# w_out's product with ELU's tile as the stationary operand: 384 and 192 moving columns in place of 512

## The chip, the cores and the metric

One core of a Trainium2 (trn2) chip. The metric is the device time of one execution in microseconds (us). Engines are named as in the profile: PE (TensorE's matmuls), PEld (its loads of stationary operands), DVE (VectorE), ACT (ScalarE), POOL (GpSimd), SP (SyncE, which issues most DMAs).

## What is computed

A softmax-weighted causal window of 7 tokens over x, head by head, then a two-layer network with ELU in between. Cut to what matters:

```
w = softmax(weight_gen, axis=-1)                  # 4 x 4096 tokens, 8 heads, 7 taps
out = einsum('bshk,bskhg->bshg', w, x_unf)        # x_unf: the last 7 tokens of x; 192 columns
x = out.reshape(16384, 192)
h = x @ w_in                                      # 192 -> 2048
g = np.where(h > 0.0, h, np.exp(np.minimum(h, 0.0)) - 1.0)
out = g @ w_out                                   # 2048 -> 192, float32
```

## The kernel before

The 16384 tokens are worked on in 32 blocks (`NB`) of 512 tokens (`N`). In a block, the 2048 inner columns are 16 tiles of 128 (`NF`), taken as 8 pairs (`NP`); one pair of one block is a step, 256 steps in all. A step does the product with w_in for its pair (two PSUM tiles `h`, one per f-tile), ELU on ACT and DVE, and, two steps later (`LAG`), the product with w_out.

Float32 accuracy at the price of fewer passes comes from splitting: x, w_in, ELU's result and w_out are each kept as a rounded part and a rest (`xhi`/`xlo`, `WI[..,0]`/`WI[..,1]`, `hi`/`lo`, the `O_HI`/`O_LO` columns of `WO`), in the type fp32r, and a product is rounded times rounded, rest times rounded and rounded times rest. Block 0 does without (`plain`): it uses float32 operands, each of whose matmuls shows as two records in the trace.

In blocks 1 to 31 (`APART`) each matmul contracts over one half of the partitions only (64 rows, `low` or `high`), and two such matmuls, one on each half, run side by side: a pair of matmuls. The product with w_in (`product_in`) is 9 matmuls of 512 columns for each of the two f-tiles. The product with w_out (`product_out`) has w_out's columns stationary and ELU's tile moving: five matmuls of 512 columns per f-tile and half, into the banks `acc` (output columns 0 to 127) and `accd` (columns 128 to 191 and the rest terms of columns 0 to 63), each half of the partitions with two banks of its own. `side` interleaves them: nine product_in matmuls of one half go beside product_out matmuls of the other. So a step is 19 pairs of matmuls of 512 columns. PSUM has eight banks: four `h`, four for the output.

When a block's sums are done, `drain` turns the four output banks over with DVE transposes (`turned`, L828), POOL adds the halves and the crossed columns (`plus`, L887), ACT copies the crossed columns (L847), and SP stores them in six DMAs of 128-byte rows (L839). Meanwhile POOL does the window sums of a later block (`conv`, L486 and L502), DVE the softmax, the transposes to `xt` and the split of x, and SP loads `wg` and `xw` (L431) and copies halves of `xhi` and `xlo` across the partitions (L634, L635).

The order on each engine is not written out: `Plan` gets every piece of work as a task with an engine, a cost, what it reads and writes and a due time, places the tasks in time and emits them in the order of their starts (`issue`). A task on the planner's "dma" engine is issued from SP's queue, in that order.

Of the kernel before, what the change touches and what calls it, by code (L numbers as in the profile page):

```python
# [52 lines left out]
class Plan:  # L53
# [7 lines left out]
    HOP = {"dma": 2200, "pe": 250, "act": 220, "dve": 220, "pool": 220}  # L61
    SAME = {"dma": 0, "pe": 0, "act": 60, "dve": 60, "pool": 60}
# [71 lines left out]
def conv_elu_kernel(  # L134
# [11 lines left out]
    nc = tc.nc  # L146
# [18 lines left out]
    D1 = D - P  # L165
# [13 lines left out]
    FIRST = (0, 2700, 5400, 12000, 18400, 28600, 38200, 44600, 51000, 56900, 62800)  # L179
# [22 lines left out]
    WO = const.tile([P, NF, 3 * P], F32R, name="WO")  # L202
    O_HI, O_BOTH, O_LO = (slice(c, c + P) for c in range(0, 3 * P, P))
    O_D = slice(P, D)
# [27 lines left out]
    r_hi = ring("hi", [P, N], 6, F32R)  # L232
    r_lo = ring("lo", [P, N], 6, F32R)
    r_cr = ring("cr", [D1, S * J, A], 1)
# [35 lines left out]
    STEP = 19 * row(N)  # L270
# [100 lines left out]
    def weights_out(k):  # L371
# [21 lines left out]
        def own(c):  # L393
            return mf()[:, :, c]

        add("act", act(n), lambda: nc.scalar.copy(out=to[:, :, 0:D], in_=own(slice(0, D))),
            reads=[m], writes=[hi_h])
        for c, hi, lo in ((slice(0, P), O_HI, O_LO), (slice(P, D), O_D, slice(D, 2 * P))):
            subtract(k in ON_VEC, nf * (c.stop - c.start), lambda lo=lo: to[:, :, lo],
                     lambda c=c: own(c), lambda hi=hi: to[:, :, hi],  # L400
                     [m, hi_h], [lo_h])
# [11 lines left out]
    def chunk(blk):  # L413
# [13 lines left out]
        def load(to, src, n, d, at=0, both=False):  # L427
            def run():
                for p, s, q in quadrants():
# [5 lines left out]
        def load_w():  # L435
            return load(lambda: w().rearrange("p t h k -> p t (h k)"), weight_gen, n, H * K,
                        both=blk == 0)

        add("dma", max(dma(P * n, H * K * 4), Q * S * ISSUE // (1 if blk else 2)), load_w(),
            writes=[wg], due=None if blk else -2)  # L440
        if blk == 0:
            xw_h[blk] = xw = [xw, Handle()]
            m = n + HALO
            for i, (a, b) in enumerate(((0, m - JH), (m - JH, m))):
                add("dma", max(dma(P * (b - a), DQ * 4), Q * S * ISSUE),
                    load(lambda a=a, b=b: xw[0].t[:, a:b], x, b - a, DQ, a),
                    writes=[xw[i]], due=-1 + i)
        else:
            add("dma", max(dma(P * (n + HALO), DQ * 4), Q * S * ISSUE),
                load(lambda: xw.t, x, n + HALO, DQ), writes=[xw])  # L450
# [130 lines left out]
    def split(blk, s0, cs):  # L581
# [49 lines left out]
        for x in (xhi, xlo) if blk else ():  # L631
            def other(x=x):
                t = x.t.bitcast(I32)
                nc.sync.dma_start(out=t[high, :, 0], in_=t[low, :, 1])  # L634
                nc.sync.dma_start(out=t[low, :, 2], in_=t[high, :, 1])  # L635

            add("dma", dma(P * C, 4 * NS) + 1250, other, writes=[x])
# [32 lines left out]
    whole = slice(0, P)  # L670

    def banks(blk, p):
        return acc_h[blk][1 if p is high else 0]

    def product_out(blk, k, p):


        acc, accd = banks(blk, p)
        out = []
        for i, f in enumerate(pair_of[k]):  # L680
            if plain(blk, k):
                half = (low, high)[i]
                for to, c in ((acc, slice(0, P)), (accd, slice(P, D))):
                    out.append(lambda f=f, to=to, c=c, i=i, half=half: nc.tensor.matmul(  # L684
                        out=to.t if to is acc else to.t[half], lhsT=w_out_f[k][1]()[:, i, c],
                        rhs=elu_h[blk, f][0].t, start=(k == 0 and (i == 0 or to is accd)),
                        stop=False, skip_group_check=True))
                continue
            hi, lo = elu_h[blk, f]
            for to, w, r in ((accd, O_BOTH, hi), (accd, O_BOTH, lo), (acc, O_HI, hi),  # L690
                             (acc, O_LO, hi), (acc, O_HI, lo)):
                def run(f=f, to=to, w=w, r=r, hi=hi, i=i):
                    nc.tensor.matmul(  # L693
                        out=to.t, lhsT=WO[p, f, w], rhs=r.t[p],
                        start=(k == 0 and i == 0 and r is hi and w != O_LO),
                        stop=(k == (NP - 2 if blk == END and p is high else NP - 1) and i == 1
                              and r is not hi), skip_group_check=True)
                out.append(run)
        if plain(blk, k):
            return [out[i] for i in (0, 2, 1, 3)]  # L700
# [27 lines left out]
    def period(s, now, up, down):  # L728
# [24 lines left out]
        if up:  # L753
            blk2, k2 = up
            if k2 == 0:
                acc_h[blk2] = [(r_acc[i].new(), r_accd[i].new())
                               for i in ((0, 1) if blk2 in APART else (0,))]
        if up and up[0] not in APART:
            if now:
                add("pe", m1, run(*pairs(t0, t1)), reads=reads, writes=h, due=due1(s))  # L760
            add("pe", 3 * pe4(N) + 200 if plain(*up) else 10 * pe(N), run(*product_out(*up, whole)), reads=ready(blk2, pair_of[k2]),
                writes=[x for y in acc_h[blk2] for x in y], due=due1(s) + 12 * pe(N))
# [4 lines left out]
        if not up and not down:  # L767
            if s == 0:
                for part in range(2):
                    t0, t1 = (product_in(blk, k, i, h[i], part) for i in range(2))  # L770
                    add("pe", C * pe4(N // 2), run(*pairs(t0, t1)),
                        reads=[*w_in_f[k][0], *xt_part[part]], writes=h, due=due1(s) + part)
            else:
                add("pe", m1, run(*pairs(t0, t1)), reads=reads, writes=h, due=due1(s))
            for f, x in zip(fs, h):
                elu(blk, f, x)
            return

        def side(mine, m2, p, hr, h, at):

            out = product_out(*m2, p) if m2 else []
            to = banks(m2[0], p) if m2 else []
            of = pair_of[m2[1]] if m2 else ()
            ahead = p is low
            for a, b, f in ((0, 5, of[0:1]), (5, 10, of[1:2])):
                todo = [x for i in range(a, b) for x in (
                    out[i:i + 1] + mine[i:i + 1] if ahead else mine[i:i + 1] + out[i:i + 1])]
                slots = b - a - (ahead and a == 0)
                add("pe", slots * row(N), run(*todo),
                    reads=[*hr, *(ready(m2[0], f) if m2 else ())],  # L790
                    writes=[*h, *to], due=due1(s) + (at + a) * pe(N))

        last = now and now == todo[-1]
        if last:
            add("pe", m1, run(*pairs(t0, t1)), reads=reads, writes=h, due=due1(s))
            for f, x in zip(fs, h):
                elu(blk, f, x)
        if now and not last:
            side(t0, up, high, reads, h[0:1], 0)
            elu(blk, fs[0], h[0])  # L800
            side(t1, down, low, reads, h[1:2], 9)
            elu(blk, fs[1], h[1])
        elif up and down:
            u, l = product_out(*up, high), product_out(*down, low)
            for i in range(2):
                add("pe", 5 * pe(N), run(*pairs(u[5 * i:5 * i + 5], l[5 * i:5 * i + 5])),
                    reads=[*ready(up[0], pair_of[up[1]][i:i + 1]),
                           *ready(down[0], pair_of[down[1]][i:i + 1])],
                    writes=[*banks(up[0], high), *banks(down[0], low)],
                    due=due1(s) + 5 * i * pe(N))  # L810
        else:
            out = product_out(*up, whole)
            for i in (0, 5, 1, 6, 2, 3, 7, 8, 4, 9):
                f = pair_of[up[1]][i // 5]
                add("pe", pe(N), run(out[i]),
                    reads=[w_out_h[f][i % 5 == 3], elu_h[up[0], f][i % 5 in (1, 4)]],
                    writes=[banks(up[0], whole)[i % 5 < 2]], due=due1(s) + i % 5 * pe(N))

    def by_token(t):
        return t.rearrange("p m w -> p (m w)")[:, 0:N].bitcast(F32).rearrange(  # L820
            "p (j a) -> p j a", a=A)

    sides = {}

    def turned(src, due):

        o = r_raw_out.new(by_token)
        add("dve", dve(N), lambda: nc.vector.transpose(  # L828
            out=o.t.rearrange("p j c -> p (j c)"), in_=src.t),
# [135 lines left out]
```

## Time and profile before

| | us |
|---|---|
| median of 3 runs | 1180.67 (1176.95 to 1181.67) |
| the profiled execution | 1177.02 |
| its span, first to last instruction | 1175.2 |
| mean granted TensorE clock | 0.998 |

The span is what the views of the trace divide up; 1.8 us of the profiled execution lie around it. A matmul's row in a timeline gives its start and a duration that includes the way to its modelled end, so two matmuls that follow each other overlap in the rows, and the time that one takes of the engine is the distance between starts.

### The profile page before, as it was taken

How to read it: one execution, taken by the hardware profiler on the slowest of the kernel's cores; microseconds unless marked ns; L12 is line 12 of the kernel's file. 1: busy time of each engine (PE TensorE's matmuls, PEld its weight loads, DVE VectorE, ACT ScalarE, POOL GpSimd, SP SyncE). 2: the span in 40 equal slices, each digit the busy share in tenths (PEclk: the TensorE clock that was granted, in tenths of full speed). 3: DMA queues.
4: the chain of work that ended last, by engine and by line, in shares of the span. 5: the costliest groups of instructions: out<-in, count | busy, mean ns of one | idle time of the engine just before them, and what ended most of it. 6: DMA issues, size and time to landing. Idle time of an engine off the chain costs nothing.

```text
span 1175.2 us, 25236 instructions
## 1 busy us (share of the span) xinstructions
PE 1166.4 (99%) x9680; PEld 920.8 (78%) x9680; DVE 888.8 (76%) x1507; ACT 949.2 (81%) x1700; POOL 798.7 (68%) x520
## 2 busy tenths in 40 slices
PE   9999999999999999999999999999999999999997
PEld 6458888888888888888888888888888888888885
DVE  7978777777778777778777777777777777777775
ACT  6768888888888888888888888888888888888785
POOL 4575766886666876666876666876666876666810
PEclk9999999999999999999999999999999999999999
DMA  9742332223332223332223331233331323311111
GB/s 192 140 73 45 69 69 46 41 55 66 69 69 43 44 54 67 69 69 40 46 55 67 69 69 38 45 57 68 69 69 36 52 53 67 69 42 30 25 39 19
DMA packets 225977, 70.60 MB, mean 60 GB/s; under 512 B 198080, under 2 KB 224704, under 8 KB 225856
## 3 DMA queue, kind: packets, MB, share of 16 engines
q1 hardware_dynamic: 223728, 68.73, 32.2%
q8 instruction: 76, 1.25, 0.5%
q10 hardware_dynamic: 2128, 0.25, 0.2%
q14 instruction: 45, 0.37, 0.1%
HBM read 31.98 MB, written 12.58 MB: 38 GB/s over the span
## 4 chain that ended last, share of the span: by engine, by line
PE 98%; SPq 1%; DMA 0%; DVE 0%; issue 0%; POOL 0%; DVEq 0%; POOLq 0%
PE h L663 46%; PE acc L693 29%; PE accd L693 20%; PE acc L684 1%; PE accd L684 1%; DMA raw_out<-in_moe_w_out 0%; SPq L349 0%; PE accd L544 0%; PE acc L544 0%; SPq L431 0%; DVE e L863 0%; POOL m_in L331 0%; DVE raw_out L828 0%; DVE m_in L321 0%; DVEq L961 0%
## 5 line engine op out<-in xcount | busy, mean ns | idle before, releaser
L663 PE MATMUL h<-xhi,WI 64*128 64x512 f32 x2976 | 766.0, 391 | 0.0
L693 PE MATMUL acc<-hi,WO 64*128 64x512 f32 x1980 | 614.9, 391 | 0.0
L663 PEld LDWEIGHTS h<-xhi,WI 64*128 64x128 f32 x2976 | 546.7, 185 | 67.9 <-DVE m_out L321 0.8
L717 DVE SCALAR_TENSOR_TENSOR h<-e,h 128x512 f32<-128x512 f32 x496 | 341.5, 694 | 259.7 <-ACT e L714 251.1
L663 PE MATMUL h<-xlo,WI 64*128 64x512 f32 x1488 | 422.0, 391 | 0.0
L712 ACT ACTIVATE e<-h 128x512 f32<-128x512 f32 x512 | 307.0, 601 | 117.3 <-PE h L663 117.3
L693 PEld LDWEIGHTS acc<-hi,WO 64*128 64x128 f32 x1980 | 364.6, 185 | 43.8
L693 PE MATMUL accd<-hi,WO 64*128 64x512 f32 x990 | 385.8, 391 | 0.0
L693 PE MATMUL accd<-lo,WO 64*128 64x512 f32 x990 | 385.7, 391 | 0.0
L693 PE MATMUL acc<-lo,WO 64*128 64x512 f32 x990 | 385.6, 391 | 0.0
L724 DVE TENSOR_TENSOR lo<-h,hi 128x512 fp32r<-128x512 f32 x496 | 335.3, 681 | 10.1 <-ACT hi L722 0.6
L722 ACT CAST hi<-h 128x512 fp32r<-128x512 f32 x496 | 287.3, 579 | 67.5 <-DVE h L717 67.2
L714 ACT ACTIVATE e<-e 128x512 f32<-128x512 f32 x512 | 323.5, 634 | 15.7
L663 PEld LDWEIGHTS h<-xlo,WI 64*128 64x128 f32 x1488 | 273.5, 185 | 32.9
L502 POOL TENSOR_TENSOR pa<-pa,pb 128x768 f32<-128x768 f32 x150 | 278.1, 1854 | 14.3 <-DVE pb L486 1.8
L486 POOL TENSOR_TENSOR pb<-xw,wg 128x768 f32<-128x768 f32 (+1 forms) x179 | 276.0, 1542 | 9.4
L486 POOL TENSOR_TENSOR pa<-xw,wg 128x768 f32<-128x768 f32 (+1 forms) x31 | 47.3, 1526 | 270.9 <-DVE wg L475 264.6
L693 PEld LDWEIGHTS accd<-hi,WO 64*128 64x128 f32 x990 | 182.2, 185 | 22.2 <-ACT e L857 0.4
L693 PEld LDWEIGHTS accd<-lo,WO 64*128 64x128 f32 x990 | 182.3, 185 | 21.9
L693 PEld LDWEIGHTS acc<-lo,WO 64*128 64x128 f32 x990 | 182.3, 185 | 21.9
L887 POOL TENSOR_TENSOR raw_out<-raw_out 128x512 f32<-128x512 f32 x60 | 77.9, 1298 | 23.5 <-DVE raw_out L828 23.5
L502 POOL TENSOR_TENSOR xc<-pa,pb 128x768 f32<-128x768 f32 x30 | 55.6, 1852 | 2.4
(91 smaller groups left out, 546.8 us busy)
## 6 DMA issues: line engine op xcount, KB each, us to landing
xw<-in_x SPq DMA_DIRECT2D x124, 168.0 KB, 4.6
out_dram<-raw_out SPq DMA_DIRECT2D x189, 64.0 KB, 2.0
xhi<-xhi SPq DMA_DIRECT2D x62, 192.0 KB, 3.2
xlo<-xlo SPq DMA_DIRECT2D x62, 192.0 KB, 3.6
wg<-in_weight_gen SPq DMA_DIRECT2D x126, 28.0 KB, 2.1
raw_out<-in_moe_w_out SPq DMA_DIRECT2D x8, 384.0 KB, 5.8
raw_in<-in_moe_w_in SPq DMA_DIRECT2D x12, 192.0 KB, 5.1
raw_in<-in_moe_w_in SPq DMA_DIRECT2D x8, 96.0 KB, 2.7
```

Source lines behind the costliest of these rows:

```text
L486: lambda: eng.tensor_tensor(out=h.t[:, 0:J], in0=xw.t[:, j0 + k:j0 + k + J, :].rearrange("p j (h g) -> p j h g", g=G), in1=wg.t[:, j0:j0 + ...
L502: add("pool", pool(J * DQ), lambda b=b, to=to: nc.gpsimd.tensor_tensor(out=to.t, in0=a.t, in1=b.t, op=ALU.add), reads=[b] if to is a else ...
L663: return lambda: nc.tensor.matmul(out=h.t, lhsT=w_in_f[k][1]()[p, c] if w is None else WI[p, k, w, c], rhs=x.t[p, c, c0:c0 + 2].rearrange( ...
L684: out.append(lambda f=f, to=to, c=c, i=i, half=half: nc.tensor.matmul(out=to.t if to is acc else to.t[half], lhsT=w_out_f[k][1]()[:, i, c] ...
L693: nc.tensor.matmul(out=to.t, lhsT=WO[p, f, w], rhs=r.t[p], start=(k == 0 and i == 0 and r is hi and w != O_LO), stop=(k == (NP - 2 if blk ...
L712: add("act", act(N, True), lambda: nc.scalar.activation(out=e.t, in_=h.t, func=ACTF.Relu, scale=-1.0), reads=[h], writes=[e])
L714: add("act", act(N), lambda: nc.scalar.activation(out=e.t, in_=e.t, func=ACTF.Exp, scale=-1.0), writes=[e])
L717: add("dve", dve(N), lambda: nc.vector.scalar_tensor_tensor(out=to.t, in0=e.t, scalar=-1.0, in1=h.t, op0=ALU.add, op1=ALU.max), reads=[e, ...
L722: add("act", act(N, True), lambda: nc.scalar.copy(out=hi.t, in_=h.t), reads=[h], writes=[hi])
L724: add("dve", dve(N), lambda: nc.vector.tensor_tensor(out=lo.t, in0=h.t, in1=hi.t.bitcast(F32), op=ALU.subtract), reads=[h, hi], writes=[lo])
L887: add("pool", pool(N), lambda: nc.gpsimd.tensor_tensor(out=to.t[0:n], in0=to.t[0:n], in1=other.t[0:n], op=ALU.add), reads=reads, writes=[t ...
```

## The change

w_out's product changes its roles. ELU's tile is now stationary, in four groups of 128 tokens (`NG`), and w_out moves: `hi` against 384 columns (both parts of w_out side by side, `2 * D`), `lo` against 192 columns (the rounded part). A result tile is 128 tokens by output columns, so nothing has to be turned over at the end of a block. In block 0 the plain product is eight matmuls of 192 columns per step.

A bank now belongs to a token group and takes sums from both halves of the partitions. The halves share the four banks in turn: while the high half works on group g, the low half works on group g+2. Where a bank passes from one half to the other, a `Turn` puts an empty instruction on SP, which waits for the old half's last matmul, and the new half's first matmul waits for it. The product is done every second step, for both pairs of f-tiles of the two steps at once: eight parts, two for each position of the groups.

`drain` is now four ACT copies of 128x192 out of PSUM, four DVE additions of the other 192 columns, and four DMAs of 768-byte rows. The rings `hi` and `lo` have seven buffers instead of six. Loads of `wg` and `xw` and the copies across partitions are planned one DMA at a time.

```diff
-    STEP = 19 * row(N)
+    def turned(n):
+        return NG * n * 288
+
+    STEP = 9 * row(N) + turned(2)
...
+    class Turn:
+        def __init__(self):
+            self.h, self.last, self.hop = Handle(), None, None
+
+        def run(self):
+            self.hop = nc.sync.nop().ins
+            tc.add_manual_dep(self.hop, self.last.name, SYNC, reason=HALVES)
...
+    def product_out(blk, k, at):
+
+
+        bank, out = acc_h[blk], []
+
+        def one(to, f, src, p, g, n, start):
+            def run():
+                w = w_out_f[k][1]()[:, f[0]] if plain(blk, k) else WO[p, f[1], 0:n]
+                return nc.tensor.matmul(out=to(), lhsT=src.t[p, g * P:(g + 1) * P], rhs=w,
+                                        start=start, stop=False, skip_group_check=True).ins
+            out.append(run)
+
+        for f in enumerate(pair_of[k]):
+            begins = k == 0 and f[0] == 0
             if plain(blk, k):
...
+            for src, n in zip(elu_h[blk, f[1]], (2 * D, D)):
+                for p, off in ((high, 0), (low, NG // 2)):
+                    g = (at + off) % NG
+                    one(lambda g=g, n=n: bank[g].t[:, 0:n], f, src, p, g, n,
+                        begins and n > D and at < NG // 2)
         return out
...
+            elif s % 2:
+                each = [(at, i) for at in range(NG) for i in range(2)]
+                if k2 == NP - 1 and blk2 == END:
+                    each = [(at, i) for a in (0, 2) for i in range(2) for at in (a, a + 1)]
+                for n, (at, i) in enumerate(each):
+                    k, after, over = k2 - 1 + i, None, None
+                    if i == 0:
+                        after = turns.get((blk2, k - 2 * (at < 2), at ^ 2))
+                    elif at < 2 or k < NP - 1:
+                        over = turns[blk2, k - 1, at] = Turn()
+
+                    def part(k=k, at=at, after=after, over=over):
+                        done = [x() for x in product_out(blk2, k, at)]
+                        if after:
+                            tc.add_manual_dep(done[0], after.hop.name, SYNC, reason=HALVES)
+                        if over:
+                            over.last = done[-1]
...
+        for g in (0, 2, 1, 3):
+            b, e = acc_h[blk][g if blk in APART else g // 2], Handle()
+            add("act", act(D, True), lambda b=b, g=g: nc.scalar.copy(
+                out=o.t[:, g], in_=b.t[:, 0:D] if blk in APART else b.t[
+                    :, g % 2 * D:(g % 2 + 1) * D]),
+                reads=[b, *([o] if parts else [])], writes=[e, *([] if parts else [o])])
+            parts.append(e)
+            if blk in APART:
+                add("dve", dve(D), lambda b=b, g=g: nc.vector.tensor_tensor(
+                    out=o.t[:, g], in0=b.t[:, D:2 * D], in1=o.t[:, g], op=ALU.add),
+                    reads=[b, o], writes=[e])
```

What stands on PE in the middle of the program before, from the start of a step's first half (`h` is product_in, L693 is product_out; a shape is the result's; what a row waits for stands in brackets):

```order
L663 MATMUL h<-xhi,WI 128x512 [waits DVE_49]
L693 MATMUL accd_8583<-hi,WO 128x512 [waits Activation_49]
L663 MATMUL h<-xhi,WI 128x512
L693 MATMUL accd_8583<-lo,WO 128x512
L663 MATMUL h<-xhi,WI 128x512
L693 MATMUL acc_8582<-hi,WO 128x512
L663 MATMUL h<-xhi,WI 128x512
L693 MATMUL acc_8582<-hi,WO 128x512
L663 MATMUL h<-xhi,WI 128x512
L693 MATMUL acc_8582<-lo,WO 128x512
```

Now the two products stand apart. This is PE at the start of a block's first two steps (L661 is product_in, L689 product_out):

```order
L661 MATMUL h<-xhi,WI 128x512 [waits DVE_49] x2
L661 MATMUL h<-xhi,WI 128x512 x10
L661 MATMUL h<-xlo,WI 128x512 x6
L661 MATMUL h<-xhi,WI 128x512 [waits DVE_49] x2
L661 MATMUL h<-xhi,WI 128x512 x10
L661 MATMUL h<-xlo,WI 128x512 x6
L689 MATMUL acc_10972<-WO,hi 128x384 [waits Activation_49]
L689 MATMUL acc_10973<-WO,hi 128x384 [waits DVE_49]
L689 MATMUL acc_10972<-WO,lo 128x192
L689 MATMUL acc_10973<-WO,lo 128x192
L689 MATMUL acc_10972<-WO,hi 128x384
L689 MATMUL acc_10973<-WO,hi 128x384
```

Two steps of product_in, 18 pairs of 512 columns, come first; then 64 narrow matmuls in a row, in pairs of 384 and of 192 columns by turns. Further down the same 64, where the halves have changed banks:

```order
L689 MATMUL accd_10995<-WO,lo 128x192
L689 MATMUL accd_10996<-WO,lo 128x192
L689 MATMUL acc_10973<-WO,hi 128x384 [waits SP_sequencer_49]
L689 MATMUL acc_10972<-WO,hi 128x384
L689 MATMUL acc_10973<-WO,lo 128x192
L689 MATMUL acc_10972<-WO,lo 128x192
```

The matmul that starts on a bank of the other half waits for SP; 434 rows of PE wait so, 14 in each of the 31 blocks. On SP the empty instructions have no rows of their own; their wait for PE is shown with the DMA behind them. SP in the middle of the program before:

```order
L431 DMA xw<-in_x 32x14x96 [waits DMAHW6_49]
L431 DMA xw<-in_x 32x14x96 [waits DMAHW7_49]
L431 DMA xw<-in_x 32x14x96 [waits DMAHW0_49]
L431 DMA xw<-in_x 32x14x96 [waits DMAHW1_49]
L431 DMA wg<-in_weight_gen 32x8x28 [waits DMAHW2_49,DVE_49,Pool_49]
```

And now (L426 loads, L633 copies across the partitions, L838 stores):

```order
L426 DMA wg<-in_weight_gen 32x8x28 [waits PE_49,DMAHW0_49]
L426 DMA xw<-in_x 32x14x96 [waits DMAHW1_49]
L426 DMA xw<-in_x 32x14x96 [waits DMAHW2_49]
L426 DMA xw<-in_x 32x14x96 [waits DMAHW3_49]
L633 DMA xhi<-xhi 64x3x256 [waits PE_49,DMAHW4_49,Activation_49]
L633 DMA xlo<-xlo 64x3x256 [waits DMAHW5_49,DVE_49,PE_49]
L633 DMA xhi<-xhi 64x3x256 [waits DMAHW6_49]
L633 DMA xlo<-xlo 64x3x256 [waits PE_49,DMAHW7_49]
L838 DMA out_dram<-raw_out 32x4x192 [waits PE_49,DMAHW0_49,DVE_49]
```

The loads and stores now stand between empty instructions that wait for PE, in one queue, and a DMA that waits for ACT, DVE or POOL holds the empty instructions behind it.

## Rows read from the trace of the kernel before

**Rows 1.** The page: busy time, share of the span and instructions by engine.

```profile
PE 1166.4 (99%) x9680; PEld 920.8 (78%) x9680; DVE 888.8 (76%) x1507; ACT 949.2 (81%) x1700; POOL 798.7 (68%) x520
```

**Rows 2.** Windows, blocks 1 to 31: length, busy PE, PEld, DVE, ACT, POOL; clock; DMA.

```profile
85.00:1160.00 1075.00, 1075.00 (x9254) 870.58 (x9254) 810.52 (x1365) 887.11 (x1579) 748.27 (x469) 1.00 0.30 55
```

**Rows 3.** The page: the chain that ended last, shares by engine.

```profile
PE 98%; SPq 1%; DMA 0%; DVE 0%; issue 0%; POOL 0%; DVEq 0%; POOLq 0%
```

**Rows 4.** What PE waited for: us in total, times, longest.

```profile
PE acc L407 <- POOL ident masks.py:199: 1.4, 1, 1.4
PE h L659 <- POOL m_in L331: 0.2, 1, 0.2
```

**Rows 5.** Groups by line and form: count, busy us, mean ns, idle before.

```profile
L663 PE MATMUL h<-xhi,WI 64*128 64x512 f32 x2976 | 766.0, 391 | 0.0
L693 PE MATMUL acc<-hi,WO 64*128 64x512 f32 x1976 | 613.6, 391 | 0.0
...
L663 PE MATMUL h<-xlo,WI 64*128 64x512 f32 x1488 | 422.0, 391 | 0.0
L693 PE MATMUL accd<-hi,WO 64*128 64x512 f32 x988 | 385.1, 391 | 0.0
```

**Rows 6.** PE's timeline: first and last pair of half-height matmuls of the split steps.

```profile
76.81 0.49 PE L663 MATMUL h<-xhi,WI 64*128 64x512 f32 x1
...
1165.16 0.40 PE L693 MATMUL acc<-lo,WO 64*128 64x512 f32 x2
```

**Rows 7.** Timeline in mid-program: a load, its neighbours, and ELU's first instruction.

```profile
602.11 0.39 PE L663 MATMUL h<-xlo,WI 64*128 64x512 f32 x1
...
602.33 0.39 PE L663 MATMUL h<-xhi,WI 64*128 64x512 f32 x1
602.33 0.18 PEld L663 LDWEIGHTS h<-xhi,WI 64*128 64x128 f32 x1
...
602.53 0.60 ACT L712 ACTIVATE e<-h 128x512 f32<-128x512 f32 x1 [0.64 <-PE h L663]
```

**Rows 8.** PEld's timeline in block 0: two loads on each half after a wait.

```profile
28.46 0.19 PEld L663 LDWEIGHTS h<-xhi,m_in 64*128 64x128 f32 x2 [0.81 <-DVE acc L318]
28.57 0.19 PEld L663 LDWEIGHTS h<-xhi,m_in 64*128 64x128 f32 x2
```

**Rows 9.** PE's timeline at the start: 128-column records back to back.

```profile
7.71 0.72 PE L407 MATMUL acc<-ident 128*128 128x128 f32 x5
```

**Rows 10.** Line 407 alone: duration of one record, least, median, greatest.

```profile
L407 PE MATMUL acc<-ident x42: 274/421/580, 1.4 to 8.6; 128*128 128x128 f32 x42
```

**Rows 11.** PE's timeline in block 0: one plain product_out, and what follows it.

```profile
25.54 1.98 PE L684 MATMUL acc<-hi,m_out 128*128 128x512 f32 x4
...
28.46 2.85 PE L663 MATMUL h<-xhi,m_in 64*128 64x512 f32 x12
```

**Rows 12.** Timeline at the end, from the last matmul on.

```profile
1167.44 0.63 PE L693 MATMUL acc<-lo,WO 128*128 128x512 f32 x2
...
1168.44 0.65 DVE L863 TENSOR_TENSOR e<-acc,e 128x512 f32<-128x512 f32 x1
1168.61 0.62 ACT L847 COPY cr<-raw_out 64x512 f32<-64x512 f32 x1 [2.37 <-DVE raw_out L828]
```

**Rows 13.** What SP's queue waited for: us in total, times, longest.

```profile
SPq L431 <- POOL pb L486: 525.6, 27, 22.0
...
SPq L634 <- ACT e L712: 111.4, 30, 7.5
```

**Rows 14.** SP's timeline in one block: DMAs issued back to back.

```profile
615.05 1.79 SPq L431 DMA_DIRECT2D wg<-in_weight_gen  x4
...
627.37 3.22 SPq L431 DMA_DIRECT2D xw<-in_x  x4
```

**Rows 15.** Groups by line: the costliest side work at a block's end.

```profile
L887 POOL TENSOR_TENSOR raw_out<-raw_out 128x512 f32<-128x512 f32 x60 | 77.9, 1298 | 23.5 <-DVE raw_out L828 23.5
```

More of the change, by code (lines that the diff above doesn't have):

```diff
@@ new lines, in conv_elu_kernel @@
+    HALVES = "a bank takes sums from one half of the rows at a time"
+    turns = {}
+    class Turn:
[4 more added lines that the diff above has]
+            tc.add_manual_dep(self.hop, self.last.name, SYNC, reason=HALVES)
+    SYNC = mybir.DependencyInfo(mybir.DependencyClass.Sync, mybir.DependencyReason.DATA)
+    def product_out(blk, k, at):
[8 more added lines that the diff above has]
+            begins = k == 0 and f[0] == 0
+            if plain(blk, k):
+                for i in range(2):
+                    one(lambda i=i: bank[at].t[:, i * D:(i + 1) * D], f, elu_h[blk, f[1]][0],
+                        slice(0, P), 2 * at + i, D, begins and i == 0)
+                continue
+            for src, n in zip(elu_h[blk, f[1]], (2 * D, D)):
[3 more added lines that the diff above has]
+                        begins and n > D and at < NG // 2)
@@ L726, in elu, with period @@
             reads=[h, hi], writes=[lo])
-    def period(s, now, up, down):
+    def period(s, now, up):
         def run(*lists):
@@ L755, in period @@
             if k2 == 0:
[L756 to L762, printed above, removed]
+                acc_h[blk2] = [r.new() for r in (r_acc[0], r_accd[0], r_acc[1], r_accd[1])[
+                    :NG if blk2 in APART else NG // 2]]
@@ new lines, in period @@
+        if up and now:
+            add("pe", m1, run(*pairs(t0, t1)), reads=reads, writes=h,
+                due=due1(s) - (s % 2 * turned(2) if s >= NP + LAG else 0))
+        if up:
+            bank = acc_h[blk2]
+            if plain(*up):
+                for at, b in enumerate(bank):
+                    add("pe", 4 * pe4(D), run(*product_out(*up, at)),
+                        reads=ready(blk2, pair_of[k2]), writes=[b],
+                        due=due1(s) + 9 * row(N) + 4 * at * pe4(D))
+            elif s % 2:
[14 more added lines that the diff above has]
+                            over.last = done[-1]
+                    add("pe", turned(2) / NG, part,
+                        reads=[*ready(blk2, pair_of[k]), *([after.h] if after else ())],
+                        writes=[bank[at], bank[at ^ 2], *([over.h] if over else ())],
+                        due=due1(s) + 9 * row(N) - turned(2) + n * turned(2) / NG)
+                    if over:
+                        add("hop", 60, over.run, writes=[over.h])
@@ L766, in period @@
             return
[L767 to L791, printed above, removed]
@@ L793, in period @@
-        last = now and now == todo[-1]
-        if last:
-            add("pe", m1, run(*pairs(t0, t1)), reads=reads, writes=h, due=due1(s))
[L796 to L817, printed above, removed]
@@ L875, in drain @@
[L875 to L897 removed]
+        parts = []
@@ new lines, in drain, with store @@
+        for g0, step in ((0, 2), (1, 2)) if end else ((0, 1),):
+            for q in range(P // A):
+                def store(q=q, g0=g0, step=step):
+                    dst = rows(out, blk * J * S, J * S)
+                    eng = nc.scalar if end and q % 2 else nc.sync
+                    eng.dma_start(out=dst[:, g0 * (P // A) + q:J * S:step * (P // A)],
+                                  in_=o.t[q * A:(q + 1) * A, g0:NG:step])
+                add("dma", max(dma(J * S * A // 4, D * 4), ISSUE), store,
+                    reads=[o, *(parts[g0 * 2:g0 * 2 + 2] if end else parts)], due=late + g0)
@@ L909, in conv_elu_kernel @@
             up = todo[s - LAG] if s >= LAG else None
-            down = up if up and up[0] in APART and up != todo[-1] else None
             if now:
```

166 lines of the change are left out of this document (41 added, 125 removed).

## Prediction

> **What bounds the kernel now.** The page's first line shows PE busy for 99% of the span, the others for 68 to 81% [rows 1]. Since a busy matmul row overlaps the next, that alone proves little, so I read three more views. The windows show PE busy for all 1075.00 of 1075.00 us from 85 on, at a granted clock of 1.00 (the level of 2.4 GHz), ACT for 887, DVE for 811, POOL for 748 [rows 2]. The chain that ended last is PE for 98% [rows 3]. PE waits for another engine only at the start, 1.6 us in all [rows 4]. So in blocks 1 to 31 the time is PE's own stream, and what PE is given to do there counts in full, until another wait appears.
>
> The unit of that stream comes from counting. product_in has 2976 + 1488 half-height matmuls, 36 of them in block 0's last two steps; product_out has 1976 + 3 x 988 [rows 5]. That is 2214 + 2470 = 4684 pairs, and their first and last starts are 76.81 and 1165.16 [rows 6]: 1088.35 / 4683 = 0.2324 us per pair of 512 columns. At 2.4 GHz 512 columns would take 0.2133, so 0.019 is overhead, per column or per matmul; the trace has no narrower fp32r matmul to tell which.
>
> **What is removed and added on PE.** product_in keeps its nine pairs per step. product_out loses ten pairs: 10 x 0.2324 = 2.324 us per step. It gets eight pairs of 384 and eight of 192 columns, by turns. Columns alone would give 8 x 576 = 4608 against 5120, a tenth less; but every pair brings a load of 128 stationary columns per half, and the short stream may be too short to hide it. I cost one long pair and one short pair together.
> - The long pair: 0.2324 x 384/512 = 0.1743 if the overhead goes with columns, 0.2324 - 128/2400 = 0.1791 if each matmul pays it. I take 0.1765.
> - The short pair's own stream would be 0.087 to 0.099. But the next load starts only when this stream starts: in mid-program the load's row begins with the matmul's, at 602.33 [rows 7]. And a load takes the array's load path for 0.11: the second loads of both halves begin 0.11 after the first, side by side [rows 8], and records of 128 columns follow each other every (0.72 - 0.274)/4 = 0.1115 [rows 9, 10]. So the short pair takes about 0.1105, set by the load and not by its columns.
>
> The two together: 0.287, with bounds 0.1743 + 0.109 = 0.283 and 0.1791 + 0.1115 = 0.291. Eight times that is 2.296 us (2.264 to 2.328) against 2.324: 0.028 us less per step, and in 248 steps **6.9 us less**, between 14.9 less and 1.0 more. The tenth of the columns is mostly eaten by weight loads.
>
> A rule of the Trainium skill (TensorE: Matmul & The Clock Gate, Part 3, "What overlaps and what doesn't") speaks against this: a load overlaps matmuls in flight only where it goes to another row group. Then each half's own stream would hide none of its loads. The rows deny it for long streams: with a load of 0.11 exposed, 512 columns could not repeat every 0.2324. By the rule the kernel would end where rival 4 puts it.
>
> **The other edits.**
> - Block 0: a plain product_out took 28.46 - 25.54 = 2.92 us, four records of 512 columns in 1.98 (0.43 each behind the first load, twice 512/2400: two passes) and then half-width ones beside each other [rows 11]. Now 16 records of two passes over 192 columns: 16 x 384/2400 + 0.11 for the first load = 2.67. That would be 8 x 0.25 = 2.0 us less were PE alone the bound there. But block 0's PE also waits for decoded weights and for products by DVE, and at its end two steps of product_in now have to come before the first w_out product, with ELU's results in bursts. I take 0, from 2 less to 2 more.
> - The end: after the last matmul (ends at 1167.44 + 0.63 = 1168.07) DVE still adds, turns over and adds again, with a copy on ACT between [rows 12], and the span ends 7.1 us after that matmul. Now two narrow copies on ACT and two narrow additions on DVE do it, each under the 0.62 and 0.65 of their 512-column kin; four of about 0.35 make 1.4 against some 2.4 before the stores. I take 0.8 less (0 to 1.5).
> - At each block's end POOL loses two additions of 1.3 us [rows 15] and more, DVE its transposes, ACT gets small copies. None of these is on the path, and the load on each falls or stays: 0. PE waits for the drained banks only after two steps of product_in, 18 x 0.2324 = 4.2 us later.
> - ELU now gets four `h` tiles within those 4.2 us, then none for 4.6. ACT was busy 83% and DVE 75% of the windows [rows 2]; they must finish four tiles per 8.77 us instead of two per 4.4. Four banks and seven buffers carry that: 0, up to 2 more.
>
> **The new wait.** A bank passes to the other half by PE, SP, PE. Between the last matmul of a position and the first that needs its bank lie two parts of the neighbouring position: 4 x 0.287 = 1.15 us. The nearest row for one signal out of PE is ELU's: the last matmul of `h` starts at 602.11 and ACT starts at 602.53 [rows 7], 0.42 less the stream's 0.23: 0.19. No row shows the way back; with as much again and some 0.05 for the instruction, 0.43 of the 1.15 are used. Cover left: 0.7. What stands ahead on SP eats it: one wg issue takes 1.79/4 = 0.45, one xw issue 3.22/4 = 0.8 [rows 14]. One hides, two in a row, or one DMA that waits for its data, do not. Behind a late empty instruction stands the matmul, and behind that all of PE. Of a block's 14 turns six have two steps of product_in to spare; eight have only the 0.7. With 16 DMAs a block I take 1 us in all, from 0 to 10.
>
> **Sum.** -6.9 (product) + 0 (block 0) - 0.8 (end) + 0 + 1.0 (turns) + 1.0 (half of what ELU's bursts may cost) = -5.7 us on the profiled execution's 1177.0 (span 1175.2 and 1.8 around it): 1171.3, or 0.48% less. That execution was 3.7 us faster than the median of the runs, 1180.67, so for the median I scale: 1180.67 x 0.9952 = **1175**.
>
> **Rivals.**
> 1. SP holds the turns up. For: SP's queue waited 525.6 us for POOL and 111.4 for ACT, up to 22.0 at once [rows 13]; it could, for nothing else stood behind. Now 14 turns per block do. Against: the order puts each DMA where its data should be ready. Price: from 0.22 us per block (6.7/31) the gain is gone; at 0.4 us it is 12.4 - 6.7 = 5.7 slower, 1186; at 0.7 us 15 slower, 1196. This is the case on the other side.
> 2. Loads cost the short pairs nothing, because they can be pulled ahead further than one. Then a long and a short pair take 0.1743 + 0.087 = 0.261, 8 x 0.261 = 2.09: 0.23 x 248 = 58 us less, 1123. Against: loads in the rows never start before the previous matmul of their half.
> 3. The load path is taken for the whole 0.18 of a load's row [rows 7]. Then the short pair is 0.18 and the long one 0.18: 8 x 0.36 = 2.88, 0.556 x 248 = 138 us more, 1318; or less, if loads run ahead. For: PEld's share of 78%. Against: rows 8 and 9, where loads repeat every 0.11. A narrow fp32r stream that runs slower per column than a wide one belongs here too; no row shows one.
> 4. Nothing overlaps within a half (the rule above): 0.1765 + 0.09 + 2 x 0.11 = 0.487, 8 x that 3.9, 1.57 x 248 = 390 us more, 1570. Against: the 0.2324.
>
> **Chances.** My forecast, a product between 14.9 less and 1.0 more with the turns mostly covered, has 0.70; its own range is 1164 to 1182. Rival 1 has 0.17, rival 2 has 0.05, rivals 3 and 4 have 0.06 and 0.02. About 0.5% (5.9 us) is what a measurement of this kernel can tell from no change. The forecast's sum lies just at it: of its 0.70, 0.35 fall beyond, 0.34 within, 0.01 on the slow side. With rival 2: faster 0.40. Of rival 1 0.08 stays within, 0.09 goes beyond: same 0.42, slower 0.09 + 0.08 + 0.01 = 0.18. The range that holds 8 in 10 leaves out rivals 2 to 4 (0.13) and the far end of rival 1: 1164 to 1187.
>
> **What would show it.** In the trace of the changed kernel: pairs of product_in still every 0.232; in the narrow stretch starts alternating about 0.177 and 0.11, with a load's row beginning at each short matmul's start (0.09 after short ones would be rival 2, 0.18 rival 3). PEld's share rises although PE's falls little. Among PE's waits, SP should be absent or below some 3 us in total; tens of us would be rival 1, and its gaps would stand before the matmul on a bank of the other half, behind SP issues. After the last matmul, 6 to 6.5 us to the span's end. I am wrong first in the sum if the alternating distance is off: each 0.001 us is 2 us of the whole.

## The result and the profile after

The changed kernel's median is 1168.66 us (1168.14 to 1168.82, 4 runs); beside it the kernel before had 1178.81 (1176.91 to 1181.67, 4 runs). The ratio is 0.9911, with a 95% interval of 0.9885 to 0.9937: 0.9% faster, where 1175 and 0.48% were forecast. Two of the four runs of the kernel before were about 4 us longer than the others; beside the experiments below its medians are 1176.8 to 1177.0, and against those the change is worth 0.7%. The profiled execution took 1168.66, 8.4 less than that of before; its span is 1166.9 against 1175.2.

The page's busy line of the changed kernel answers to [rows 1], the window over blocks 1 to 31 to [rows 2] (length, busy PE, PEld, DVE, ACT and POOL, clock, DMA), and the chain's first line to [rows 3]:

```profile
PE 1159.8 (99%) x12730; PEld 1041.2 (89%) x12730; DVE 828.8 (71%) x1501; ACT 894.7 (77%) x1794; POOL 689.8 (59%) x424
```

```profile
85.00:1158.00 1073.00, 1072.90 (x12214) 978.19 (x12212) 759.49 (x1367) 836.10 (x1674) 640.71 (x377) 1.00 0.25 55
```

```profile
PE 97%; SPq 1%; DVE 1%; DMA 1%; issue 0%; POOL 0%; DVEq 0%; ACT 0%; POOLq 0%
```

PE is still the bound, at a granted clock of 1.00, and has 0.10 us without work in 1073. PEld's share rose from 78% to 89%, ACT's, DVE's and POOL's fell. So the gain has to be found in PE's own stream and at its two ends. The chain in order of time gives the length of two steps (start, us, engine, tile, line, count):

```profile
850.37 4.21 PE h L661 x36
859.15 4.21 PE h L661 x36
```

From one row's start to the next, two steps now take 8.78 us; before, 38 pairs of 0.2324 took 8.831. That is 0.051 less, 124 times, 6.3 us. PE's timeline in the narrow stretch shows how (start, us):

```profile
600.22 0.25 PE L689 MATMUL accd<-WO,lo 64*128 64x192 f32 x2
600.22 0.19 PEld L689 LDWEIGHTS accd<-WO,hi 64*128 64x128 f32 x2
600.30 0.36 PE L689 MATMUL accd<-WO,hi 64*128 64x384 f32 x2
600.33 0.19 PEld L689 LDWEIGHTS accd<-WO,lo 64*128 64x128 f32 x2
600.50 0.25 PE L689 MATMUL accd<-WO,lo 64*128 64x192 f32 x2
```

From short pair to short pair it is 0.287 (the rows round it to 0.28). The load for the next long pair starts with the short one, at 600.22; the long pair's row starts at 600.30, but the next load follows at 600.33, 0.11 behind the first. The long matmul's row includes 0.02 of waiting for its weights: starts alternate by 0.199 and 0.087, not by 0.177 and 0.11, and the sum is the same.

What PE and PEld waited for, of PE all its groups but the first 1.4 us [rows 4], of PEld two further groups (us in total, times, longest):

```profile
PE accd L542 <- DVE v L555: 0.6, 1, 0.6
PE h L657 <- POOL m_in L331: 0.2, 1, 0.2
...
PEld h L661 <- DVE lo L728: 0.7, 2, 0.4
```

```profile
L689 PEld LDWEIGHTS acc<-WO,hi 64*128 64x128 f32 x1984 | 192.8, 185 | 5.5 <-SPq L676 0.2
L689 PEld LDWEIGHTS accd<-WO,hi 64*128 64x128 f32 x1984 | 190.9, 184 | 0.2 <-SPq L676 0.2
```

Of 434 turns over SP (L676) two held PE up, by 0.2 us each. ELU's bursts show at one place, 0.7 us around 632. At the end stand these rows, which answer to [rows 12], and behind the dots two rows of the kernel before that [rows 12] leave out:

```profile
1162.01 0.25 PE L689 MATMUL accd<-WO,lo 64*128 64x192 f32 x2
1162.08 0.62 DVE L829 TENSOR_TENSOR raw_out<-acc,raw_out 128x192 f32<-128x192 f32 x2 [3.42 <-ACT raw_out L823]
1162.30 0.54 ACT L823 COPY raw_out<-accd 128x192 f32<-128x192 f32 x2
1162.65 0.62 DVE L829 TENSOR_TENSOR raw_out<-accd,raw_out 128x192 f32<-128x192 f32 x2
1162.73 1.73 SPq L838 DMA_DIRECT2D out_dram<-raw_out  x4
1162.73 1.81 ACTq L838 DMA_DIRECT2D out_dram<-raw_out  x4
...
1169.20 0.71 DVE L828 STREAM_TRANSPOSE raw_out<-e 128x512 f32<-128x512 f32 x1
1169.83 0.64 DVE L869 TENSOR_TENSOR raw_out<-raw_out,cr 64x512 f32<-64x512 f32 x1
```

The next two views are of the stretch from 1159 to the end, first after, then before: GB/s in slices of 0.5 us, packets, and the last block's stores with count, KB each and median us from issue to landing. Both kernels send them from two queues, SP's and ACT's. The last row of each is the page's, for the stores in mid-program, from SP's queue alone.

```profile
GB/s 0 0 0 0 0 0 0 0 57 204 211 202 92 0 0 0 0 0 0 0 0 0 0 0 0 0 0 0 0 0 0 0 0 0 0 0 0 0 0 0
DMA packets 641, 0.40 MB, mean 19 GB/s; under 512 B 128, under 2 KB 640, under 8 KB 640
...
out_dram<-raw_out SPq DMA_DIRECT2D x4, 48.0 KB, 1.6
out_dram<-raw_out ACTq DMA_DIRECT2D x4, 48.0 KB, 1.8
...
out_dram<-raw_out SPq DMA_DIRECT2D x124, 96.0 KB, 1.9
```

```profile
GB/s 0 0 0 0 0 0 31 0 0 0 0 0 0 0 0 0 0 0 0 0 0 0 71 130 122 129 143 152 3 0 0 0 0 0 0 0 0 0 0 0
DMA packets 3169, 0.41 MB, mean 20 GB/s; under 512 B 3168, under 2 KB 3168, under 8 KB 3168
...
out_dram<-raw_out SPq DMA_DIRECT2D x3, 64.0 KB, 2.8
out_dram<-raw_out ACTq DMA_DIRECT2D x3, 64.0 KB, 3.1
...
out_dram<-raw_out SPq DMA_DIRECT2D x189, 64.0 KB, 2.0
```

From the end of the last stream (1162.01 + 0.09) to the span's end are 4.8 us; before they were 7.3, from 1167.9 on (two matmuls of 0.23 after 1167.44 [rows 12]). Behind the last stream stood two transposes, two additions and a copy of 512 columns, until 1170.47, for 2.6 us; now two copies and four additions of 192 columns end at 1163.27, 1.2 us behind it. The stores land 1.6 to 1.8 us behind their issue in place of 2.8 to 3.1.

The account of the 8.3 us of span: 0.5 by the end of block 0 (the split steps begin at 76.33, before at 76.81 [rows 6]), 6.3 in 124 pairs of steps, 2.5 behind the last matmul; against that about 1.0 of new waits (two turns of 0.2 and the 0.7 at 632).

### The profile page after: what moved, and what is told of

It reads as the page before. It is cut to its first block, busy times and chain, and to the rows that moved or that the text cites. A ratio compares the mean times of both kernels' runs of the same rounds, so it can differ in the third digit from the quotient of the medians.

```text
span 1166.9 us, 32082 instructions
## 1 busy us (share of the span) xinstructions
PE 1159.8 (99%) x12730; PEld 1041.2 (89%) x12730; DVE 828.8 (71%) x1501; ACT 894.7 (77%) x1794; POOL 689.8 (59%) x424
## 4 chain that ended last, share of the span: by engine, by line
PE 97%; SPq 1%; DVE 1%; DMA 1%; issue 0%; POOL 0%; DVEq 0%; ACT 0%; POOLq 0%
PE h L661 46%; PE acc L689 25%; PE accd L689 25%; DMA raw_out<-in_moe_w_out 1%; SPq L349 0%; PE accd L542 0%; SPq L426 0%; DVE m_in L321 0%; PE acc L542 0%; DVE lo L728 0%; POOL m_in L331 0%; DVE hi L721 0%; DVE raw_out L829 0%; DVE h L721 0%; DVE v L555 0%
## 5 line engine op out<-in xcount | busy, mean ns | idle before, releaser
L716 ACT ACTIVATE e<-h 128x512 f32<-128x512 f32 x512 | 278.7, 596 | 190.1 <-PE h L661 189.9
L661 PE MATMUL h<-xhi,WI 64*128 64x512 f32 x2976 | 393.1, 394 | 0.1
L661 PEld LDWEIGHTS h<-xhi,WI 64*128 64x128 f32 x2976 | 274.6, 185 | 55.1 <-DVE lo L728 0.7
L689 PE MATMUL accd<-WO,hi 64*128 64x384 f32 x1984 | 305.7, 357 | 0.0
L689 PE MATMUL acc<-WO,hi 64*128 64x384 f32 x1984 | 304.3, 355 | 0.0
L689 PE MATMUL acc<-WO,lo 64*128 64x192 f32 x1984 | 255.0, 249 | 0.0
L689 PE MATMUL accd<-WO,lo 64*128 64x192 f32 x1984 | 254.3, 248 | 0.0
L661 PE MATMUL h<-xlo,WI 64*128 64x512 f32 x1488 | 215.0, 390 | 0.0
L689 PEld LDWEIGHTS acc<-WO,lo 64*128 64x128 f32 x1984 | 194.4, 187 | 5.0
L689 PEld LDWEIGHTS acc<-WO,hi 64*128 64x128 f32 x1984 | 192.8, 185 | 5.5 <-SPq L676 0.2
L689 PEld LDWEIGHTS accd<-WO,lo 64*128 64x128 f32 x1984 | 194.6, 188 | 0.0
L689 PEld LDWEIGHTS accd<-WO,hi 64*128 64x128 f32 x1984 | 190.9, 184 | 0.2 <-SPq L676 0.2
L661 PEld LDWEIGHTS h<-xlo,WI 64*128 64x128 f32 x1488 | 142.5, 184 | 30.9
```

What stands on the lines that cost most here:

```text
L661: return lambda: nc.tensor.matmul(out=h.t, lhsT=w_in_f[k][1]()[p, c] if w is None else WI[p, k, w, c], rhs=x.t[p, c, c0:c0 + 2].rearrange( ...
L689: return nc.tensor.matmul(out=to(), lhsT=src.t[p, g * P:(g + 1) * P], rhs=w, start=start, stop=False, skip_group_check=True).ins
L716: add("act", act(N, True), lambda: nc.scalar.activation(out=e.t, in_=h.t, func=ACTF.Relu, scale=-1.0), reads=[h], writes=[e])
```

## Experiments

The theory: a long and a short pair take 0.287 because the load of the next 128 stationary columns (0.109) starts with the short stream and outlasts it; the turns cost nothing as long as 1.15 us of other work lies between; the rest of the gain is at the end. Rivals: the narrow matmuls have a price of their own, by columns or by instruction; or SP's queue decides.

### More and fewer columns for the rest

```diff
-            for src, n in zip(elu_h[blk, f[1]], (2 * D, D)):
+            for src, n in zip(elu_h[blk, f[1]], (2 * D, 240)):
```

and the same with 128 and with 384. 240 and 384 add products of rest and rest to the result; 128 leaves out a part of the rest's product.

> The rest's matmuls take 240 moving columns in place of 192 (48 columns of rest times rest are added to the result; nothing else changes). Theory: a long and a short pair together are 0.2866 us because the next load of 128 stationary columns starts with the short stream and takes 0.109; 240 columns at 0.4539 ns take 0.109 too, so the set stays at 0.287 to 0.290 and the time at 1169 to 1174. Rival, the short pair's price goes with its columns: 48 x 0.454 ns x 1984 sets = 43 us more, 1212.

> The rest's matmuls take 128 moving columns in place of 192: the product of the rest with output columns 128 to 191 is left out. Theory: the load still takes 0.109 behind the short matmul's start, so the set stays at 0.2866 and the time within 3 us of 1168.7, although a ninth of the product's columns is gone. Rival, columns count: 64 x 0.454 ns x 1984 = 58 us less, 1111.

> The rest's matmuls take 384 moving columns, as the others do (rest times rest is added). All 16 pairs of a step are long ones, whose streams cover a load, so the distance of their starts measures a long pair by itself. Theory: 0.1743 to 0.1791 us each, two of them 0.349 to 0.358 in place of 0.2866, 124 to 142 us more: about 1300. If the long pair really takes the 0.199 that stands between the recorded starts now, two take 0.398 and the time is 1390. If the overhead is per matmul, 0.179; if per column, 0.174.

Measured: 240 columns 1169.02 us (1168.68 to 1169.69), 128 columns 1168.32 (1167.84 to 1168.89), 384 columns 1296.30 (1295.96 to 1296.81). From 128 to 240 columns the time hardly moves with the columns; 0.7 us lie between, where the columns alone would make 101. With 384 it is 127.6 more than in the changed kernel, which makes 0.176 for each long pair. PE with 240 columns:

```profile
600.05 0.28 PE L689 MATMUL accd<-WO,lo 64*128 64x240 f32 x2
600.05 0.19 PEld L689 LDWEIGHTS accd<-WO,hi 64*128 64x128 f32 x2
600.16 0.33 PE L689 MATMUL accd<-WO,hi 64*128 64x384 f32 x2
...
600.33 0.27 PE L689 MATMUL accd<-WO,lo 64*128 64x240 f32 x2
```

Here the stream is as long as the load, nothing waits within a row, and the starts alternate by 0.11 and 0.17 to 0.18 as forecast for 192. With 384 columns the rows repeat every 0.17 to 0.18:

```profile
602.00 0.36 PE L689 MATMUL acc<-WO,hi 64*128 64x384 f32 x2
...
602.18 0.36 PE L689 MATMUL acc<-WO,lo 64*128 64x384 f32 x2
...
602.36 0.36 PE L689 MATMUL acc<-WO,hi 64*128 64x384 f32 x2
```

### Fewer stationary columns

```diff
-                    g = (at + off) % NG
-                    one(lambda g=g, n=n: bank[g].t[:, 0:n], f, src, p, g, n,
-                        begins and n > D and at < NG // 2)
+                    g, m = (at + off) % NG, P if n == D or begins else 96
+                    one(lambda g=g, n=n, m=m: bank[g].t[0:m, 0:n], f, src, p, g, n,
+                        begins and n > D and at < NG // 2, m)
```

This cuts the tile of the rounded part (`m` bounds the stationary columns; the other 32 tokens of each group are left out of that product, so the result is not complete); its counterpart cuts that of the rest (`P if n > D else 96`).

> The stationary tile of ELU's rounded part is cut from 128 to 96 tokens in 15 of 16 f-tiles (the other 32 tokens of each group are left out of the 384-column product); moving columns and the number of matmuls stay. Theory: this is the load that starts with the short stream; with 96 columns it takes 0.109 x 96/128 = 0.082, less than the short stream's 0.087, so the set falls to 0.264 to 0.268 and the time by 35 to 42 us, to about 1130. Rival, a fixed price of a matmul or a load whatever its columns: unchanged, 1168.7.

> The stationary tile of ELU's rest is cut from 128 to 96 tokens (its product is left out for the other 32 of each group), that of the rounded part stays whole: the counterpart to the cut that gave 33 us. Theory: this load runs under the long stream of 0.1755, which covers 0.109 as well as 0.082, so nothing changes: 1166 to 1170. Rival, any shorter load is a gain, wherever it stands: some 33 us less, 1135.

Measured: with the rounded part cut 1135.85 us (1135.39 to 1136.84), 32.8 less; with the rest cut 1167.64 (1167.59 to 1168.16), 1.0 less. Only the load that starts with the short stream counts; the one under the long stream is hidden whether it takes 0.109 or less. The first kernel's rows:

```profile
600.15 0.25 PE L689 MATMUL acc<-WO,lo 64*128 64x192 f32 x2
600.15 0.16 PEld L689 LDWEIGHTS acc<-WO,hi 64*96 64x96 f32 x2
600.23 0.34 PE L689 MATMUL acc<-WO,hi 64*96 64x384 f32 x2
...
600.41 0.25 PE L689 MATMUL acc<-WO,lo 64*128 64x192 f32 x2
```

A set takes 0.26 to 0.27, a long stream of 0.176 and a short one of 0.087 and hardly more. Two steps took 8.48, 0.30 less; 124 times that would be 37. Some 4 to 5 us of it went to the first f-tile of each block, which keeps 128, and to new waits. The Trainium skill (TensorE: Matmul & The Clock Gate, Part 2, "Step-by-step: what each phase is for") says that a load's time goes with its columns and not with its rows; this case agrees: with 96 columns the load's row fell from 0.19 to 0.16, and over 128 rows in place of 64 (next experiment) it is 0.19 again.

### No halves, no turns

```diff
-                for p, off in ((high, 0), (low, NG // 2)):
-                    g = (at + off) % NG
-                    one(lambda g=g, n=n: bank[g].t[:, 0:n], f, src, p, g, n,
-                        begins and n > D and at < NG // 2)
+                one(lambda n=n: bank[at].t[:, 0:n], f, src, slice(0, P), at, n,
+                    begins and n > D)
```

> w_out's product is done at full height: one matmul over 128 rows in place of each pair over 64, on the same bank for all rows, so no bank changes hands and there are no turns and no empty instructions on SP. Theory: the array takes a 128-row load and stream as it takes two 64-row ones beside each other; a long and a short matmul are 0.287 again, and only the 0.4 us of turns go: 1167 to 1169. Rival A, a load hides only behind matmuls on other rows, and here there are none: 0.1755 + 0.087 + 2 x 0.109 = 0.48 for the two, 0.194 x 1984 = 385 us more, 1554. Rival B, changing between 64 and 128 rows costs a drained array twice in two steps: some 0.1 to 0.2 us, 248 times, 25 to 50 us more.

Measured: 1212.43 us (1211.16 to 1213.12), 44 more. The theory fails here and rival B holds. PE at one end of the narrow stretch and at the other:

```profile
601.06 0.86 PE L661 MATMUL h<-xlo,WI 64*128 64x512 f32 x6
601.85 0.19 PEld L689 LDWEIGHTS acc<-WO,hi 128*128 128x128 f32 x1 [0.36 <-ACT e L716]
601.85 0.44 PE L689 MATMUL acc<-WO,hi 128*128 128x384 f32 x1
...
602.13 0.25 PE L689 MATMUL acc<-WO,lo 128*128 128x192 f32 x1
...
606.43 0.25 PE L689 MATMUL accd<-WO,lo 128*128 128x192 f32 x1
...
606.61 1.66 PE L661 MATMUL h<-xhi,WI 64*128 64x512 f32 x12
```

Inside, short to short is 0.287 as with halves. But from 64 to 128 rows the load's row starts only with its own matmul's, at 601.85; that matmul starts 0.32 behind the last of product_in instead of 0.233, and the next 0.284 behind it instead of 0.199. On the way back it is 0.18 from 606.43 to 606.61 instead of 0.087, and 0.1 more for the second. Two steps take 9.14 us in place of 8.78, and 124 times 0.36 is 45. The profile puts the first gap down to ACT (L716), but that is an exponential of a later tile; ACT's last casts of `hi` had started at 596.34 and taken 1.24. The gaps stand at both changes of height, and 115 of the 124 periods of two steps are 9.14 us, which a wait for other engines would hardly repeat. So the halves and their turns are worth 44 us in this kernel: with both products in halves the height never changes. What in the change of height makes the gaps is not shown. Rival A, a load that lies bare behind every matmul, would have made it 1554, and the 0.287 at full height speaks against it. The Trainium skill (TensorE: Matmul & The Clock Gate, Part 3, "What overlaps and what doesn't") states the rule behind that rival, that a load overlaps matmuls in flight only where it goes to another row group; this trace does not agree, for here all matmuls of the stretch are on the same 128 rows and a set still takes 0.287.

### The turns laid bare, and SP's queue

```diff
-                each = [(at, i) for at in range(NG) for i in range(2)]
+                each = [(at, i) for at in (0, 2, 1, 3) for i in range(2)]
```

> The order of the four positions is 0, 2, 1, 3 in place of 0, 1, 2, 3, so that two of the four bank changes of each two steps follow the other half's last matmul at once, with nothing between. This measures the way PE, SP, PE by itself. Theory (0.19 to SP, 0.05 there, 0.19 back): a gap of 0.43 us at some 248 places, 107 us more, 1276, the gaps on PE waiting for SP; with 0.2 each 50 us, with 0.8 each 200. If the way back to the matmul costs nothing that can be seen, or the turns are done on PE itself, no change. The 1.15 us of cover in the changed kernel are then the reason that its 434 turns cost 0.4 us.

Measured: 1266.40 us (1265.77 to 1269.51), 97.7 more. One turn in PE's timeline, and PEld's waits for SP (us in total, times, longest):

```profile
603.03 0.25 PE L689 MATMUL acc<-WO,lo 64*128 64x192 f32 x2
603.37 0.19 PEld L689 LDWEIGHTS acc<-WO,hi 64*128 64x128 f32 x2 [0.33 <-SPq L676]
603.37 0.45 PE L689 MATMUL acc<-WO,hi 64*128 64x384 f32 x2
...
603.66 0.25 PE L689 MATMUL acc<-WO,lo 64*128 64x192 f32 x2
```

```profile
PEld acc L689 <- SPq L676: 47.9, 123, 1.3
PEld accd L689 <- SPq L676: 45.4, 123, 1.4
```

Two steps with two bare turns repeat every 9.47 us, 0.69 more than 8.78: 0.35 for each turn, 85 us in all; PEld's waits say 0.37 to 0.39 on average. The other 12 or 13 us are turns that found SP busy: 28 matmuls on a new bank start over 0.4 us behind the pair before, and in each case an issue of a DMA on SP ended 0.11 us before the start. Of the 0.35, 0.25 lie between the end of the last stream (603.03 + 0.087) and the next matmul's start, and 0.09 behind it, since the load starts only with that matmul (0.29 to the next start in place of 0.199). So the way PE, SP, PE itself is 0.25, where 0.43 was estimated. The records of SP's empty instructions (in most turns 0.28 behind the last short pair's start) split it: 0.19 to SP, as ELU's row had given, but only 0.06 from there to PE.

Two edits let SP interfere: the loads planned in fours again (as before the change), and the product done every step for one pair of f-tiles.

```diff
-        for one in quadrants() if blk else ():
-            add("dma", max(dma(A * n, H * K * 4), ISSUE), load_w([one]), writes=[wg])
+        else:
+            add("dma", max(dma(P * n, H * K * 4), Q * S * ISSUE), load_w(), writes=[wg])
```

(and so for `xw` and the copies across the partitions)

```diff
-            elif s % 2:
-                each = [(at, i) for at in range(NG) for i in range(2)]
+            else:
+                each = [(at, 0) for at in range(NG)]
```

> The loads of wg and xw are again planned four DMAs at a time, and the copies across the partitions two at a time; all else stays. Theory (my first rival): four issues in a row keep SP's queue for 1.8 and 3.2 us, longer than the 1.15 us of cover, so the turns behind them come late: where they fall into the narrow stretch, a gap of 0.6 to 2 us each, 10 to 40 us more in all, with PE waiting for SP's queue. Rival: the planner still finds room for them beside two steps of product_in (4.2 us without a turn), and the time stays within 2 us of 1168.7.

> w_out's product is done in every step for its one pair of f-tiles, not in every second step for two pairs. The streams are the same; a bank change now has one part of the neighbouring position between, 0.573 us in place of 1.147, and a block has 30 of them in place of 14. Theory: the bare way over SP takes 0.35 to 0.38, so 0.2 us of cover are left, and a turn behind one DMA issue of 0.45 comes late; with 16 DMAs a block, some of them in the stretch, 5 to 25 us more: 1174 to 1194. Rival: the planner keeps SP free there, and without bursts of ELU it is 0 to 1 us less: 1168.

Measured: in fours 1176.07 us (1174.66 to 1179.89), 7.4 more and level with the kernel before (ratio 0.9996, interval 0.9987 to 1.0006); every step 1171.25 (1170.86 to 1172.44), 2.6 more. PE's waits for SP's queue, with the loads in fours (there the lines have numbers one lower) and with the product in every step:

```profile
PE accd L688 <- SPq L675: 3.8, 6, 1.3
PE acc L688 <- SPq L675: 1.7, 4, 0.6
```

```profile
PE acc L689 <- SPq L676: 2.0, 5, 0.7
```

With the loads in fours ten turns of 434 came late, and that ate the gain: PE's own waits make 5.5 us, those of its loads for SP 7.9. All ten matmuls start 0.11 to 0.12 us behind the end of an issue of `wg` or `xw`. The loss is less than the 10 to 40 forecast, since most turns were still on time. With half the cover and twice the turns the loss is smaller than the 5 to 25 expected too: five of PE's 930 turns came late.

### Rings and the last store

```diff
-    r_hi = ring("hi", [P, N], 7, F32R)
-    r_lo = ring("lo", [P, N], 7, F32R)
+    r_hi = ring("hi", [P, N], 6, F32R)
+    r_lo = ring("lo", [P, N], 6, F32R)
```

```diff
-        end = blk == END
+        end = False
```

> Six buffers each for ELU's rounded part and rest, as before the change, in place of seven. Theory: ELU's third and fourth tile wait for the end of the narrow stretch, but some 3 us of slack are left before the next one starts, so PE shows less than 3 us of waits for ELU and the time stays at 1168 to 1172. Rival: the bursts need the seventh buffer; a wait of 0.3 us in every two steps would be 37 us more.

> The last block is stored as all others are: four DMAs on SP once all four groups are done, in place of two sets of four on SP's and ACT's queues by turns. Theory: part of the 2.5 us that the tail gained comes from this, four issues in a row take 1.7 us from the last addition on, so the tail grows from 4.8 to 5.4 us (5.0 to 6.3) and the time to 1169.3. Rival: the whole 2.5 come from this, 1171.2; or nothing, 1168.7.

Measured: 1168.91 us (1168.80 to 1169.23) with six buffers and 1168.98 (1168.70 to 1169.61) with one set of stores. The seventh buffer is worth nothing here. With one set the last matmul starts at 1161.53 and the span ends at 1167.3: a tail of 5.7 us in place of 4.8, so without two sets on two queues the tail is 0.9 longer; PE happened to end 0.5 earlier, which hides half of it in the time, and the 0.3 that are left are no more than runs differ. This is no share of the 2.5 that the tail gained: the kernel before, too, stored its last block in two sets from both queues. With one queue the 96 KB stores landed in a median of 1.9.

## Why the prediction was right

**The product.** Forecast 6.9 less, measured 6.3. The set was put at 0.287 and is 0.287; the long pair at 0.1765 and is 0.176; the short pair is set by the load, which three column counts and the two cut tiles show. Rivals 2 to 4 fall with the same runs: a load is not hidden behind the short stream, is not taken for its row's 0.19, and does overlap within a half. Only the picture in the rows was drawn wrong, 0.199 and 0.087 in place of 0.177 and 0.11, because part of the wait lies within the long matmul's row. One reading was weaker than it was taken for: the float32 records of [rows 9, 10] repeat every 0.1115, but at 0.43 per 512 columns [rows 11] their streams alone would take 0.107, so they can't tell a load from a stream; [rows 8] and the cut tiles carry the 0.11.

**The turns.** Taken as 1.0, measured 0.4. The 0.43 for the way over SP is 0.25, or 0.35 with the load behind it, and the 1.15 us cover it. Rival 1 is real and was kept away by the planning of single DMAs: with the loads in fours 7.4 us, 0.24 a block, were lost, and nothing was left of the gain; 0.22 a block had been named as that point.

**ELU's bursts** were taken as 1.0; 0.7 us of waits stand in the trace, once. **Block 0** was taken as 0; it ends 0.5 earlier, inside its bounds.

**The end** is the mis-sized term: 0.8 less (0 to 1.5) was taken, 2.5 was measured. The prediction counted copies and additions and left out the stores. The stores' way from issue to landing is 1.6 to 1.8 us in place of 2.8 to 3.1, some 1.2 us, and the work up to the last issue gave the other 1.3. That the packets made the landing faster (640 for the stores, 128 of them under 512 B, in place of 3168, all under 512 B) was read from the trace and not tried by itself. For it speaks the rate: with both queues issuing, 0.4 MB moved at 202 to 211 GB/s in the full slices after and at 122 to 152 before. The short rows alone are not enough: in mid-program, from one queue, the kernel before's stores landed in 2.0, no later than those of 96 KB now.

Together: 0.6 too much for the product, 0.9 too much for waits, 0.5 too little for block 0 and 1.7 for the end, 2.5 to 2.7 of gain not forecast. That the errors of the product and of the waits partly cancel is luck. Of the 6.3 by which the median lies below the forecast of 1175, the other 3.7 come from scaling that up to the median of three runs, 1180.67.

## What to carry to other kernels

Fewer moving columns pay only down to the time of the next load: between 128 and 240 columns of fp32r on 128 stationary ones the column count did not matter here, and the stationary tile that is loaded behind the short stream did. A hand-over of a bank through another engine's queue cost 0.35 us where it lay bare and next to nothing with 1.15 us of other work between, as long as no burst of DMA issues stood ahead in that queue. Keep one partition split for products that alternate: changing between 64 and 128 rows cost 0.36 us there and back.

## What the runs showed of the hardware

- The change of height cost 0.36 us for going there and back, while 128-row and 64-row streams run at the same 0.287 per set on their own.
- 48 more columns for the rest, in 1984 sets, cost 0.4 us in all, no more than runs differ: what fitted under a load was free.
- PE, SP, PE by empty instructions adds 0.35 us to the normal distance of two matmuls: 0.25 for the way and 0.09 for the load that then lies bare.
- Issued from two queues at once, stores of 64 KB in 128-byte rows landed in 2.8 to 3.1 us, stores of 48 KB in 768-byte rows in 1.6 to 1.8; from one queue in mid-program, stores of 64 KB in 128-byte rows landed in 2.0 and stores of 96 KB in 768-byte rows in 1.9. The Trainium skill (DMA: Bandwidth & Descriptors, Specifications) names 512 B as the least size of a transfer at line rate; the rates at the end agree (122 to 152 GB/s with the short rows, 202 to 211 with the long ones), and the stores in mid-program show no difference.
